# Attention and squared-ReLU layer on one core: the second layer's quarters as a chain in one PSUM region, batch 1's first layer by seven products, and a new order

## The chip, the cores and the metric

The kernel runs on one core of one Trainium2 chip. The metric is the device time of one execution in microseconds; of several runs the median is taken. A profile comes from one execution of its own, and its span goes from the first to the last instruction of the core.

## The reference

Four batches of 768 tokens, eight heads of 64. Each token attends to the last 128 tokens and to the first four ("sinks"); the 512 numbers that come out go through two layers with a squared ReLU between.

```
scores = scale * q @ k.T                       # scale = 1/sqrt(64)
keep   = (pos_k < 4) | (0 <= pos_q - pos_k < 128)
a      = softmax(where(keep, scores, -1e9))
x      = concat_heads(a @ v)                   # [3072, 512]
h      = x @ w_in                              # [512, 2048]
g      = max(h, 0) ** 2
out    = g @ w_out                             # [2048, 512], float32
```

## The kernel before

The work is cut by batch (0 to 3), and each batch of 768 tokens into three slices (or pairs) of 256 tokens. For each batch the kernel loads q, k and v (`qn`, `qr`, `v`), transposes q and k into `qkT` (on TensorE as `pt` for batches 0 and 1; for batches 2 and 3, named `NATURAL`, by DMA "turns" that SP issues), computes scores `ps` (L600, L607), exponentials `expm` on ScalarE (L628), triangle masks on POOL (`domask`, L215), values `po` (L676), normalises them into `xn_sb` (L693), and transposes them into `xT` (L725). Then follow two layers.

**First layer** in its plain form (`layer1`, L757): each block of 128 of the 2048 hidden columns is four matmuls over the depth of 512, `pm`; a relu (L768 on ScalarE, L770 on VectorE) and a square into `gT_sb`. Batches 0 and 1 are done so.

**First layer by seven products** (`layer1_fast` and `quad`, L887), for batches 2 and 3: the depth, the hidden columns and the tokens are each halved, and the eight half-products are replaced by seven of sums and differences (Strassen's scheme). Tokens' sums are `xs` (L845), weights' sums `wi` (L803; two of them are written into `w_in_sb` itself, L811, after the plain layers are through). A quad takes its seven products in one two-bank `pm`, with a copy `t`, two subtractions (L928), a relu (L943), a saturated sum with a floor at zero (L955) and two squares (L909, L911). `FAST = (2, 3)` names the batches.

**Second layer** in its plain form (`layer2`, L976) for pairs (0,0) and (0,1), given as (batch, pair); and by seven products (`layer2_fast`, L1086) for the ten other pairs. Here the two tiles of 128 tokens, the two halves of the 2048 and the two halves of the 512 output columns are the halves. Four sums of `gT_sb` blocks are made on VectorE (`total`, L1044: s1 to s4), four of `w_out_sb` once (`wt`). The seven products p1 to p7 (eight matmuls of 256 columns each) go into four half banks a, b, c, d of two PSUM banks; five additions behind them give the four quarters of `osb`:

- p5 goes to c, is copied into `osb` (x), and p7 in d is added to that (`pair_sum`, L1111)
- p1 goes to a and is copied into `u`; p6 goes to b, and is added to u (L1111)
- x + u is one quarter (L1127); p3 is added in c and p4 in d on the PE, and u is added to both (`middle`, L1134)
- p2 is added to a, which is copied out.

The last pair, (3,2), has a tail form of it with halved copies and stores.

**The order.** Every operation is entered in a plan with the operations it must follow and the buffers ("rooms", `Slot`) it takes. `ORDER` then lists all by number, in the order in which they are issued; a letter names the engine where there is a choice (d VectorE, a ScalarE, g POOL), and `+0`, `+1` the kind of room. Each engine takes its instructions in that order. `DUMMIES` adds matmuls without use ahead of a few operations near the start. PSUM has two rooms of two banks named `att` and two named `den`; the SBUF rooms of the pools `qr`, `qs`, `expm`, `r`, `osb`, `sg`, `u` are few: five `qr`, three `r`, two `osb`, four `sg`, two `u`. `touch` declares which PE and non-PE accesses to one two-bank tile lie in other banks, so that they don't wait for each other.

`load_natural` loads batches 2 and 3 into `qr` rooms and turns them by DMA. `weight_sums_in` makes the `wi`, which live in two of the `qr` rooms for good.

Of the kernel before, what the change touches and what calls it, by code (L numbers as in the profile page):

```python
# [21 lines left out]
0 7 8 9 1 5 10 11 2 12 13 3 14 15 55d 57+0 16 19 59a 20 17 56d 21 18 61d 63+0 22 58 62d 65a 60d 64 6 67a 83+1 79 66a  # L22
68d 69+1 85 70 71d 103+0 84+0 105 73g 74d 72d 23 75+1 86 76 77d 91+0 78a 24 87+1 93 25 89 88 92+0 80 26 114+1 90 94
95+0 4 96 117 97 106g 99+1 98 104+0 107 100d 101 118g 81+1 102d 113+0 108d 156 115 127 27 28 29 30 31 32 33 34 35 36
37 38 116d 82 109+0 111 39 40 41 119+1 121 157a 158a 110 112 120 122 162 123+1 125 163d 168 169d 126a 124a 171 172a
170a 159 160d 177 128 131 165 173d 161d 132d 178d 166d 164a 130a 129a 133a 144 146 136 138 174 145 137 289 290 148
134 175a 140 135 176a 147d 167d 139d 291 179d 292 293 141d 142 143 149g 42 43 44 45 46 150 151 47 48 49 50 51 52 53
54 365 366 367 368 208g 369 370 371 372 373 294 295 152 154 296 153d 155d 297d 298d 186 187d 180 181a 200+0 204+1
192+0 201 193 205 194a 206d 195a 189 207d 182d 203a 196+0 197 183 198a 190a 191a 188d 199d 202d 274 212+0+0 184d 209
278 279 215 213 237+0+0 210+1 211 238 240 185d 300 301 275 214 302 241d 276 277 303 280 281 282 304 219+0+0 283 222  # L30
220 306a 305 307 230+0+0 309a 233 231 308 311 223 216 221 310 239d 224+0 312 234g 232g 299 385 386 384 383 313 225
314 242+0 217+0 243 218 284 315 316 235+0 236 285 251+0 286a 287a 317d 252d 253d 244+0 246 226+1 228 247d 227d 245a
248+1 229a 399 322 249d 250d 402 400 323d 355 401 256+0+0 259 257 340 254+0 255 341a 258d 358 356 342a 396 260d 334
335a 374 375 376 377 378 379 380 381 395g 388 390 387 288 392 391 318 389 393 394 331 263+0+0 332a 261+1 264 266 319
262 267d 324d 406 333a 407 320a 337 409 265g 382 597 268+0 598 599 600 601 602 603 604 605 606 607 608 609 610 338a
321d 403 269 328 627d 410 270+0 272 404 408 329a 271a 273d 359 325 405 339a 336a 326a 346 347d 357 327a 415 418 419d
330d 352 411 353a 416 412 354d 447 448 343 344a 345a 349 422 423 425 417g 426g 611 451 452 397 363 449 453d 350d 398
450 351a 348a 454 455 457 466 456a 438 458 459 441 439 467 485 486 489 490 487 460 488 461 361 492 431 491a 432 434
615 413 616 622 620 619 493 462 494d 468 463 464a 414 465 621 617 618 420 440g 612 424g 427 496 433g 442g 428 498
421 470 471 443 435g 436 472a 504a 495 362 499 497 500 473 444 437 508 505 469 628 501 475d 474 477 647 429 625 445  # L40
430 446 650 502a 648 624 503 623 626 360 476 478 481 507 479 506 480 364 482 483d 523+0 525a 524 631 527 526 528 634
632 509+0 510 529 511d 512 530 531a 654 538 633 539 513 514 515 655 533 534 657 649g 656g 516 517a 638 613 614 535
635 536d 537 641 519 520 532a 636 658g 651g 521 639 569+0 570 637 571a 629 583+0 630 572 573 585a 640 522a 518a 574
584 587 575 576 586 555+1 642 589 577a 588 643 679 557a 540 556 590 559 591a 592a 578a 558 560 579 580 593 594 581
561 562 595 541+0 542 683 563a 564a 543d 545 544 680 546 565 547 566 548 684 686 644 567 685a 596a 549a 582a 681
550d 689 682 645 484 646 670 551 552 687 690 673 671 674g 553 688a 554a 663 691 694 666 664 665g 568d 698 692 693
699 659 652 702 703 705 667g 672g 695 696d 700 653 717 660 718 721 668 697 661 736a 704a 669 737 675 676 701 722 739
740 738 708 677 678 662 755+1 706 709 741+1 742 757a 719 720 756 743a 723a 707d 759 745 724 758 761 725 744 760 762
763a 764a 711 746 727 710 713 726a 765 766 747 712 769 714 771 767 728 730 715d 772 748 749a 729 815+0 816 817a 732
770 731 818 733 819 751 752 787+1 734a 735 716 801+0 802 803a 789a 753 820 804 768d 821 788 822 773+1 805 791 754a  # L50
823a 824a 775a 790 806 750d 792 829 807 774 793 776 825 808 794 826 809a 827 830 831 795a 796a 810a 777 779 811 778
812 797 798 833 780 834 836 813 799 828a 835a 781a 832 838d 839 783 784 782a 800a 814a 837 840 841 844 785 786d 842
848 849 852 853 855 843 845 846d 867 854a 850 851 858 857d 868 871 847 856 859 873a 861 862 860 863 864 869 872 865a
866 870 877 874 876a 875 878 880 881 886 879 882 883 885 884
# [59 lines left out]
def kernel(  # L114
# [81 lines left out]
    def touch(t, e, ins, *banks, alone=False):  # L196

        before = touched.setdefault(t, [])
        for e_, ins_, banks_, alone_ in before:
# [3 lines left out]
        before.append((e, ins, banks, alone))  # L203
# [178 lines left out]

    def load_natural(b, s, older_values):
# [36 lines left out]
    def attention(b, key):  # L420
# [3 lines left out]
        begun = [ops["layer1", b - 1, 0, 0]] if b >= 2 and b not in NATURAL else []  # L424
# [12 lines left out]
        def stage(g, f0, f1, side):  # L437
# [100 lines left out]
            if g == 0:  # L538
                def sink_keys(e):
                    for h2 in range(2):  # L540
                        r = slice(64 * h2, 64 * h2 + 64)
                        nc.vector.tensor_copy(
                            out=kb[r, :].rearrange("p (m c) -> p m c", c=136)[:, :, 4 * h2:4 * h2 + NSINK],
                            in_=qkT_sb[r, :, 1, 0, 0:NSINK])
# [11 lines left out]
                A["sink_keys"] = op(at(0.1), {"dve": 0.34}, sink_keys,  # L556
# [189 lines left out]
    def layer1(b, key, fbs, c0, cw, need):  # L746
# [3 lines left out]
        bs, rs = Slot("den", 1), Slot("r", 1)  # L750
# [10 lines left out]
        ops["layer1", b, fbs[0], c0] = a  # L761

# [51 lines left out]
    def layer1_fast(b, ss, key, step):  # L814
# [15 lines left out]
        if len(ss) == 1:  # L830
            landed = [op(key(0) - 0.012, {"act": 1.06, "dve": 1.2}, spread, after=landed, takes=[whole])]
# [28 lines left out]
    def quad(b, ss, qd, key, xs, sums, slots, part, landed, whole):  # L860
# [15 lines left out]
        def product(name, bk, n, fresh, after):  # L876
# [19 lines left out]
            ops["layer1", b, (f0, name), ss[0]] = o  # L896
            return o
# [19 lines left out]
        m1 = product(1, 0, 0, True, [o for x, o in ops.items() if x[0] == "layer1" and x[1] == b - 1])  # L917
# [43 lines left out]
    def layer2(b, u, keys, by_part=False):  # L961
        P.group = ("l2", b, u)
        bs = Slot("den", 2)
# [57 lines left out]
    def layer2_fast(b, u, key):  # L1021
# [33 lines left out]
        bs, os_, us = Slot("den", 1 if tail else 2), Slot("osb", 1), Slot("u", 1)  # L1055
        ys = Slot("att", 1) if tail else bs
# [84 lines left out]
        pairs = out[128 * g:128 * g + 256, :].rearrange("(i p) m -> p i m" if b in FAST and u else "(p i) m -> p i m", i=2)  # L1141
# [23 lines left out]
        def store_rest(e):  # L1165
            o = bank_t["osb", b, u]
            if b not in FAST or not u:
# [15 lines left out]
    NATURAL, TURNED, BIASED, FAST = (2, 3), (), 1, (2, 3)  # L1183
# [24 lines left out]
    for b in range(B):  # L1208
        if b == 0:
# [3 lines left out]
            at(1, 0.2, 0.725, "att")  # L1213
# [4 lines left out]
        elif b in FAST:  # L1218
            layer1_fast(b, (0,), lambda i, b=b: b + 0.167 * i / 2, 0.01)
            layer1_fast(b, (1, 2), lambda i, b=b: b + 0.167 + 0.34 * i / 4, 0.01)  # L1220
        else:
            for i, fb in enumerate(range(0, NFB, 2)):
                layer1(b, b + 0.34 * i / 8, (fb, fb + 1), 0, 512, (0, 1))
        for i, fb in enumerate(range(0, NFB, 4) if b not in FAST else ()):
            if b == 0:
                layer1(b, 0.2 + 0.226 * i / 4, range(fb, fb + 4), 512, 256, (2,))
            else:
                layer1(b, b + 0.34 + 0.167 * i / 4, range(fb, fb + 4), 512, 256, (2,))
        if b + 1 == FAST[0]:
            weight_sums_in(b + 0.4, [ops[x] for x in ops if x[0] == "layer1" and x[1] == b])  # L1230
        if b + 1 < B:
# [7 lines left out]
            else:  # L1239
                attention(b + 1, lambda f, b=b: b + LO + (HI - LO) * f)(0, 0.0, 1.0, "att")  # L1240
        if b == 0:
            weight_sums(0.6, [w_out_op[i] for i in range(4)])
        for u in range(NS):
            if b == 0 and u < 2:
# [40 lines left out]
```

## Time and profile before

| what | value |
|---|---|
| median of 3 runs | 213.55 us (212.48 to 214.01) |
| profiled execution: span | 210.2 us, 5719 instructions, mean TensorE clock 0.997 |
| TensorE busy | 201.4 us (96%) |
| VectorE, ScalarE, POOL busy | 170.8, 126.6, 101.8 us |
| DMA | 26.09 MB in 93881 packets, mean 124 GB/s |
| first scores of batch 2 | at 72.7 us |
| batch 1's first layer | 73.1 to 99.6 us, between other work |
| pair (0,2)'s second layer begins | at 58.7 us |

The profiled execution has no time beside its span; the span lies 3.35 us under the median of the runs and 2.3 under the fastest. Busy time counts each instruction from its start to its modelled end, so neighbouring matmuls overlap in their records: eight matmuls of 256 columns stand 0.87 us from the next group, though one has a mean of 273 ns. Idle time of an engine other than the bounding one costs nothing by itself.

### The profile page before, as it was taken

Reading aid. Unit: us, or ns where it says so; the run is one execution under the profiler, and the core shown is the slowest. Engines: PE = TensorE matmul, PEld = TensorE weight load, DVE = VectorE, ACT = ScalarE, POOL = GpSimd, SP = SyncE. Lnnn points to the kernel's source line nnn. Section 1 sums busy time; section 2 is a strip of 40 time slices with the busy share of each in tenths; the row PEclk is TensorE's granted clock in tenths of the full one; section 3 lists DMA queues with packets and bytes.
Section 4 is the critical chain, followed back from the end, with each engine's and each line's share of the span. In section 5 each row is a group of like instructions: output and inputs, shape, how many; then the busy total and the mean of one; then the engine's idle time right before and its main releaser. Section 6 shows DMA issues by size and latency. Waiting matters only on the chain.

```text
span 210.2 us, 5719 instructions
## 1 busy us (share of the span) xinstructions
PE 201.4 (96%) x2383; PEld 169.4 (81%) x2383; DVE 170.8 (81%) x317; ACT 126.6 (60%) x162; POOL 101.8 (48%) x143
## 2 busy tenths in 40 slices
PE   3999999999999999999999999799999999999993
PEld 3859996689468845679789988699899999999892
DVE  7487567366999964789997988999989978999863
ACT  2498287407744579898952268889870244896110
POOL 7999774898877941999369023700253000000000
PEclk9999999999999999999999999999999999999998
DMA  5999999999999999999987639700512300400222
GB/s 171 278 188 206 171 201 214 161 155 205 153 112 157 104 150 252 138 124 144 149 102 151 103 77 179 50 3 0 150 62 69 75 5 38 166 0 0 103 100 100
DMA packets 93881, 26.09 MB, mean 124 GB/s; under 512 B 86816, under 2 KB 91552, under 8 KB 93856
## 3 DMA queue, kind: packets, MB, share of 16 engines
q0 software_dynamic: 69248, 12.59, 81.3%
q1 hardware_dynamic: 24424, 13.07, 27.9%
q8 instruction: 18, 0.29, 0.6%
q10 hardware_dynamic: 184, 0.07, 0.1%
q14 instruction: 7, 0.06, 0.1%
HBM read 27.30 MB, written 6.29 MB: 160 GB/s over the span
## 4 chain that ended last, share of the span: by engine, by line
PE 94%; DVE 2%; ACT 1%; POOL 1%; issue 1%; POOLq 0%; DVEq 0%
PE py L1086 29%; PE pm L757 20%; PE pm L887 17%; PE po L676 7%; PE py L976 7%; PE ps L607 6%; PE pt L500 3%; PE pt L182 2%; PE px L725 1%; ACT expm L628 1%; PE ya L1086 1%; PE ps L600 1%; PE pk L566 1%; DVE r L955 1%; DVE gT_sb L911 0%
## 5 line engine op out<-in xcount | busy, mean ns | idle before, releaser
L215 POOL TENSOR_SCALAR_AFFINE_SELECT expm<-expm 128x512 bf16<-128x512 bf16 x42 | 29.2, 724 | 49.5 <-ACT expm L628 24.5
L628 ACT ACTIVATE expm<-ps 128x1024 bf16<-128x1024 f32 (+1 forms) x48 | 43.8, 950 | 12.4 <-PE ps L607 11.3
L757 PE MATMUL pm<-xT,w_in_sb 128*128 128x256 bf16 (+1 forms) x320 | 44.7, 294 | 0.0
L757 PEld LDWEIGHTS <-w_in_sb 128*128 128x128 bf16 x320 | 34.2, 114 | 6.6 <-issue 0.9
L1086 PEld LDWEIGHTS <-gT_sb 128*128 128x128 bf16 x336 | 31.1, 98 | 4.2 <-issue 0.5
L1086 PEld LDWEIGHTS <-sg 128*128 128x128 bf16 x240 | 22.8, 98 | 3.3 <-issue 0.5
L768 ACT ACTIVATE r<-pm 128x1024 bf16<-128x1024 f32 x14 | 14.3, 1022 | 13.5 <-PE pm L757 13.4
L887 PEld LDWEIGHTS <-w_in_sb 128*128 128x128 bf16 x256 | 21.8, 114 | 0.5 <-issue 0.2
L887 PE MATMUL pm<-xs,wi 128*128 128x128 bf16 (+1 forms) x192 | 19.5, 246 | 1.5 <-DVE xs L845 0.9
L1086 PE MATMUL py<-wt,gT_sb 128*128 128x256 bf16 x160 | 20.8, 273 | 0.0
L1086 PE MATMUL py<-wt,sg 128*128 128x256 bf16 x160 | 20.6, 273 | 0.0
L909 ACT ACTIVATE gT_sb<-r 128x1024 bf16<-128x1024 bf16 x18 | 18.4, 1051 | 0.3
L1086 PE MATMUL py<-w_out_sb,gT_sb 128*128 128x256 bf16 x144 | 18.5, 273 | 0.0
L189 ACT ACTIVATE osb<-py 128x256 f32<-128x256 f32 (+1 forms) x15 | 6.2, 410 | 20.3 <-DMA out_dram<-osb 6.0
L770 DVE TENSOR_SCALAR r<-pm 128x1024 bf16<-128x1024 f32 x10 | 12.2, 1222 | 7.5 <-PE pm L757 4.3
L887 PEld LDWEIGHTS <-wi 128*128 128x128 bf16 x192 | 16.4, 113 | 2.2 <-issue 2.1
L693 DVE TENSOR_TENSOR xn_sb<-po,rc 128x512 bf16<-128x512 f32 (+1 forms) x28 | 17.2, 615 | 1.0
L676 PEld LDWEIGHTS <-expm 128*128 128x128 bf16 x352 | 16.3, 97 | 1.4 <-issue 0.5
L676 PE MATMUL po<-v,expm 128*128 128x65 bf16 x352 | 17.3, 193 | 0.1
L943 ACT ACTIVATE r<-pm 128x1024 bf16<-128x1024 f32 x12 | 12.1, 1021 | 8.1 <-PE pm L887 7.9
L928 DVE TENSOR_TENSOR t<-t,pm 128x512 f32<-128x512 f32 x24 | 15.9, 680 | 0.9 <-ACT t L189 0.4
L955 DVE CUSTOM_DVE_ANT_1 r<-pm,t 128x1024 bf16<-128x1024 f32 x12 | 14.5, 1220 | 1.6 <-PE pm L887 1.5
(97 smaller groups left out, 381.9 us busy)
## 6 DMA issues: line engine op xcount, KB each, us to landing
out_dram<-osb SPq DMA_DIRECT2D x11, 512.0 KB, 4.5
v<-in_v_dram POOLq DMA_DIRECT2D x24, 128.0 KB, 7.1
qn<-in_k_dram POOLq DMA_DIRECT2D x20, 128.0 KB, 7.1
qn<-in_q_dram POOLq DMA_DIRECT2D x20, 128.0 KB, 6.9
w_in_sb<-in_moe_w_in_dram POOLq DMA_DIRECT2D x4, 512.0 KB, 10.2
w_out_sb<-in_moe_w_out_dram POOLq DMA_DIRECT2D x4, 512.0 KB, 10.4
qr<-in_k_dram SPq DMA_DIRECT2D x4, 256.0 KB, 5.1
qr<-in_q_dram SPq DMA_DIRECT2D x4, 256.0 KB, 4.8
```

The source lines that it names most:

```text
L215: nc.gpsimd.affine_select(out=e_tile, in_=e_tile, compare_op=ALU.is_ge, fill=fill, base=i - 1, pattern=[[0, n], [1 if i else -1, 128]], ch ...
L628: nc.scalar.activation(out=x[:, :, o:512], in_=bank_t["s", b, s, m][:, :, o:512], func=AF.Exp, scale=scale)
L676: touch(("po", b, s, m0), e, nc.tensor.matmul(pv[:, i, h2, :], lhsT=lhsT, rhs=rhs, start=(n_ == 0), stop=(n_ == len(mms) - 1)), j)
L693: touch(("po", b, s, m0), e, nc.vector.tensor_tensor(out=xn_sb[:, 2 * s:2 * s + 2, 128 * (m0 + j0):128 * (m0 + j0 + nj)].rearrange("p i (j ...
L757: nc.tensor.matmul(pm[:, i, :], lhsT=w_in_sb[:, fb // 4, kb, fb % 4:512:4], rhs=xT[:, c0 // 256:(c0 + cw) // 256, kb, :], start=(kb == 0), ...
L768: nc.scalar.activation(out=o, in_=h, func=AF.Relu)
L887: touch(tag, e, nc.tensor.matmul(y[:, bk, i, :], lhsT=weights(name, f0 + i, a), rhs=rhs[:, a, :], start=fresh and i == 0 and a == 0, stop= ...
L909: nc.scalar.activation(out=d, in_=x, func=AF.Square)
L928: touch(tag, e, nc.vector.tensor_tensor(out=T["t"], in0=T["t"], in1=T["y"][:, bk], op=ALU.subtract), bk)
L955: touch(tag, e, nc.vector._custom_dve(TENSOR_ADD_SAT, out=r.rearrange("p b n c -> p b (n c)"), in0=T["y"].rearrange("p b n c -> p b (n c)" ...
L976: touch((b, u), e, nc.tensor.matmul(pm[:, i, :], lhsT=gT_sb[:, fb, 128 * t:128 * t + 128], rhs=w_out_sb[:, fb, :], start=(fb == 0), stop=( ...
L1086: ins = nc.tensor.matmul(y_, lhsT=x[:, i, :], rhs=r_, start=(first or tail and n == 2) and i == 0, stop=i == HB - 1, skip_group_check=not ...
```

## The change

- Nine of the ten fast pairs get a new form of the second layer, `layer2_chain`; the last pair keeps `layer2_fast`. The same seven products are taken. p1 goes into a half bank r and is copied to the first quarter of `osb`; p6 is accumulated on it and the sum copied to the third; p5 is accumulated and the sum copied to the fourth; p3 is accumulated and the sum copied to the second. p7, then p4, go to half bank d, p2 to half bank a (both in the other bank), and three additions put them onto the quarters. The buffer `u`, L1127 and L1134 are gone for these pairs.
- Batch 1's first layer goes by seven products as well (`FAST` now names, per batch, the slices taken together). Its `wi` are therefore made earlier, after batch 0's first layer, and take their two `qr` rooms from then on.
- All two-bank PSUM users may take either kind of room, `att` or `den`.
- The sink keys are copied by ScalarE where the order says so, before always by VectorE; the spread of a lone slice is on ScalarE only.
- Loads of batches 2 and 3 follow the first operation of the first layer two batches earlier, whichever that is; only those of batch 3 must follow the first `wi`. Attention no longer waits in the plan for the first layer one batch earlier.
- `ORDER` is new: 944 entries for 887. It is left out below.

```diff
-    def touch(t, e, ins, *banks, alone=False):
+    def touch(t, e, ins, *banks, alone=False, part=None):
...
-            apart = (e == "pe") != (e_ == "pe") or e != e_ and alone and alone_
+            apart = (e == "pe") != (e_ == "pe") or e != e_ and alone and alone_ and (part is None or part != part_)
...
-        begun = [ops["layer1", b - 2, 0, 0], w_out_op[3]]
+        begun = [first_layer1[b - 2], w_out_op[3]]
...
-                if b - 1 in FAST:
+                if b == 3:
                     o.after += [ops["wi", 1, 0]]
...
-        begun = [ops["layer1", b - 1, 0, 0]] if b >= 2 and b not in NATURAL else []
+        begun = []
...
-                        nc.vector.tensor_copy(
-                            out=kb[r, :].rearrange("p (m c) -> p m c", c=136)[:, :, 4 * h2:4 * h2 + NSINK],
-                            in_=qkT_sb[r, :, 1, 0, 0:NSINK])
+                        copy(e, kb[r, :].rearrange("p (m c) -> p m c", c=136)[:, :, 4 * h2:4 * h2 + NSINK],
+                             qkT_sb[r, :, 1, 0, 0:NSINK])
...
-                A["sink_keys"] = op(at(0.1), {"dve": 0.34}, sink_keys,
+                A["sink_keys"] = op(at(0.1), {"act": 0.42}, sink_keys,
...
-        bs, rs = Slot("den", 1), Slot("r", 1)
+        bs, rs = Slot(("den", "att"), 1), Slot("r", 1)
...
-        m1 = product(1, 0, 0, True, [o for x, o in ops.items() if x[0] == "layer1" and x[1] == b - 1])
+        m1 = product(1, 0, 0, True, [])
...
+    def layer2_chain(b, u, key):
...
+        o1 = total("s1", a21, a22, ALU.add, s1_, key(0), low + high, [])
+        o3 = total("s3", a11, a21, ALU.subtract, None, key(0), low + [o1], [])
+        o2 = total("s2", "s1", a11, ALU.subtract, s2_, key(0), [o1], [s1_])
+        o4 = total("s4", a12, "s2", ALU.subtract, s4_, key(0), [o2], [s2_])
+
+        bs, os_ = Slot(("den", "att"), 4), Slot("osb", 1)
+        w = lambda half, cols: w_out_sb[:, HB * half:HB * half + HB, 256 * cols:256 * cols + 256]
+        HOME = {"r": (0, 0), "d": (1, 0), "a": (1, 1)}
...
+                for i in range(HB):
+                    touch((b, u), e, nc.tensor.matmul(region(name), lhsT=x[:, i, :], rhs=w_[:, i, :],
+                                                      start=first and i == 0, stop=i == HB - 1,
+                                                      skip_group_check=not first), HOME[name][0])
...
+                d = bank_t["osb", b, u][:, q, :]
+                if add:
+                    ins = nc.vector.tensor_tensor(out=d, in0=region(of), in1=d, op=ALU.add)
+                else:
+                    ins = copy(e, d, region(of))
+                touch((b, u), e, ins, HOME[of][0], alone=True, part=q)
...
+        p1 = product(0, "r", a11, w(0, 0), True, low, takes=[bs])
+        p7 = product(1, "d", "s3", 3, True, [o3, ops["wt", 3]], [p1])
+        c1 = quarter(0, "r", 0, [p1], False, takes=[os_])
+        p6 = product(2, "r", "s2", 2, False, [o2, ops["wt", 2], c1], reads=[s2_])
+        c2 = quarter(2, "r", 2, [p6], False)
+        p5 = product(3, "r", "s1", 1, False, [o1, ops["wt", 1], c2], reads=[s1_])
+        c3 = quarter(3, "r", 3, [p5], False)
+        p2 = product(4, "a", a12, w(1, 0), False, high, [p7])
+        e1 = quarter(0, "a", 4, [p2, c1], True, reads=[bs])
+        e4 = quarter(3, "d", 4, [p7, c3], True)
+        p3 = product(5, "r", "s4", w(1, 1), False, [c3, o4], reads=[s4_])
+        p4 = product(6, "d", a22, 4, False, [e4, ops["wt", 4]] + high)
+        e2 = quarter(1, "r", 5, [p3], False, reads=[bs])
+        e3 = quarter(2, "d", 6, [p4, c2], True, reads=[bs])
...
-    NATURAL, TURNED, BIASED, FAST = (2, 3), (), 1, (2, 3)
+    CHAIN = True
+    NATURAL, TURNED, BIASED = (2, 3), (), 1
+    FAST = {1: ((0, 1), (2,)), 2: ((0,), (1, 2)), 3: ((0,), (1, 2))}
+    CLASSIC2 = ((0, 0), (0, 1))
...
+        if done and 1 not in {x[1] for x in ops if x[0] == "wi"}:
+            weight_sums_in(b + 0.4, [o for x, o in ops.items() if x[0] == "layer1"])
...
-                layer2_fast(b, u, lambda n, u=u, b=b: b + 0.5 + 0.5 * (8 * u + 8 * n / 7.0) / 24)
+                (layer2_chain if CHAIN and (b, u) != (B - 1, NS - 1) else layer2_fast)(
+                    b, u, lambda n, u=u, b=b: b + 0.5 + 0.5 * (8 * u + 8 * n / 7.0) / 24)
```

More of the change, by code (lines that the diff above doesn't have):

```diff
@@ L27 @@
[L27 to L36, printed above, removed]
@@ L830, in layer1_fast @@
         if len(ss) == 1:
-            landed = [op(key(0) - 0.012, {"act": 1.06, "dve": 1.2}, spread, after=landed, takes=[whole])]
+            landed = [op(key(0) - 0.012, {"act": 1.06}, spread, after=landed, takes=[whole])]
         else:
@@ L1053, in layer2_fast @@
         o4 = total("s4", a12, "s2", ALU.subtract, s4_, key(0), [o2], [s2_])
-        bs, os_, us = Slot("den", 1 if tail else 2), Slot("osb", 1), Slot("u", 1)
-        ys = Slot("att", 1) if tail else bs
+        bs, os_, us = Slot(("den", "att"), 1 if tail else 2), Slot("osb", 1), Slot("u", 1)
+        ys = Slot(("att", "den"), 1) if tail else bs
         w = lambda half, cols: w_out_sb[:, HB * half:HB * half + HB, 256 * cols:256 * cols + 256]
@@ L1139, in layer2_fast @@
         g = NT * b + 2 * u
-        pairs = out[128 * g:128 * g + 256, :].rearrange("(i p) m -> p i m" if b in FAST and u else "(p i) m -> p i m", i=2)
+        natural = any(u in ss and len(ss) == 2 for ss in FAST.get(b, ()))
+        pairs = out[128 * g:128 * g + 256, :].rearrange("(i p) m -> p i m" if natural else "(p i) m -> p i m", i=2)
         def rows(i, c0, c1):
```

148 lines of the change are left out of this document (108 added, 40 removed).

## The prediction

> **What bounds the kernel now.** I read the page's busy shares first, then the chain that ended last, then the waits of TensorE, then the stages in windows, and last the groups by line for prices.
>
> ```profile
> PE 201.4 (96%) x2383; PEld 169.4 (81%) x2383; DVE 170.8 (81%) x317; ACT 126.6 (60%) x162; POOL 101.8 (48%) x143
> ...
> PE 94%; DVE 2%; ACT 1%; POOL 1%; issue 1%; POOLq 0%; DVEq 0%
> ```
>
> ```profile
> PE pt L182 <- POOL ident L239: 3.5, 1, 3.5
> PE pm L887 <- DVE xs L845: 0.9, 1, 0.9
> PE pm L887 <- ACT r L943: 0.7, 1, 0.7
> ```
>
> ```profile
> 16.80:72.70 55.90, 55.87 (x652) 44.97 (x654) 42.11 (x73) 29.95 (x41) 44.61 (x58) 1.00 1.84 167
> 72.70:100.10 27.40, 27.40 (x278) 18.49 (x278) 20.56 (x39) 24.39 (x29) 19.44 (x25) 1.00 2.16 161
> 100.10:123.90 23.80, 23.80 (x309) 20.43 (x308) 21.78 (x45) 12.39 (x17) 10.23 (x14) 1.00 1.02 119
> 123.90:166.40 42.50, 40.96 (x562) 37.55 (x561) 40.15 (x70) 30.22 (x38) 12.88 (x18) 1.00 0.38 75
> ```
>
> ```profile
> L757 PE MATMUL pm<-xT,w_in_sb 128*128 128x512 bf16 x64 | 15.1, 381 | 0.0
> ...
> L943 ACT ACTIVATE r<-pm 128x1024 bf16<-128x1024 f32 x12 | 12.1, 1021 | 8.1 <-PE pm L887 7.9
> L928 DVE TENSOR_TENSOR t<-t,pm 128x512 f32<-128x512 f32 x24 | 15.9, 680 | 0.9 <-ACT t L189 0.4
> L955 DVE CUSTOM_DVE_ANT_1 r<-pm,t 128x1024 bf16<-128x1024 f32 x12 | 14.5, 1220 | 1.6 <-PE pm L887 1.5
> L1044 DVE TENSOR_TENSOR sg<-gT_sb 128x1024 bf16<-128x1024 bf16 x10 | 7.5, 748 | 0.6 <-ACT gT_sb L909 0.5
> L1134 DVE TENSOR_TENSOR osb<-py,u 128x512 f32<-128x512 f32 x10 | 6.9, 689 | 3.3 <-PE py L1086 3.2
> L189 ACT ACTIVATE osb<-py 128x256 f32<-128x256 f32 (+1 forms) x15 | 6.2, 410 | 20.3 <-DMA out_dram<-osb 6.0 <-DVE osb L1134 5.3 <-PE py L976 5.0
> L1127 DVE TENSOR_TENSOR osb<-osb,u 128x256 f32<-128x256 f32 x10 | 5.1, 506 | 0.1
> L1111 DVE TENSOR_TENSOR u<-py,u 128x256 f32<-128x256 f32 x10 | 4.2, 419 | 1.9 <-PE py L1086 1.8
> ```
>
> TensorE is 96% busy and is the chain. The waits answer (total, times, longest) leaves 1.6 us inside the body, both in batch 2's first layer: 0.7 at 131.6 and 0.9 at 133.9. Another 3.5 stand ahead of the first matmul and 3.5 behind the last. In the windows (length, then the busy time of PE, PEld, DVE, ACT, POOL) TensorE is unbroken from 16.8 to 123.9. So a microsecond of products taken out is a microsecond of time, unless something else makes TensorE wait. VectorE is next: it has 40.15 of 42.5 in the stage where the two waits stand, and 20.56 of 27.4 in batch 1's first layer (72.7 to 100.1), the stage that the change makes heavier. In the groups the two last numbers before the idle column are busy time and mean ns; records of neighbouring matmuls overlap, so I price matmuls by the time from one group to the next: eight of 256 columns 0.87, sixteen of 256 1.75, eight of 512 1.73, eight of 128 0.44.
>
> The profiled span is 210.2. The median of the runs, 213.55, lies 3.35 over it; I carry that 3.35 unchanged.
>
> **The change, part by part.**
>
> *Batch 1's first layer by seven products.* Before it is 64 matmuls of 512 columns and 64 of 256 (L757): 64 x 0.216 + 64 x 0.109 = 21.0 us. Seven products of half the blocks and half the depth do 7/8 of that: 18.4. **TensorE: -2.6.** Every price is proportional to columns, so nothing is lost to the smaller shapes.
>
> It is paid for behind TensorE. Each of the six quads (four over two slices, two over one) needs one copy of 0.6 (L189, on ScalarE for five of them), two subtractions of 0.68, one saturated sum of 1.22, one relu of 1.02 and two squares of 1.05. VectorE in this layer: 6 x 1.22 + 12 x 0.68 + 3.4 for the input sums + 0.7 + two squares 1.4 = 21.0, against three relus (3.7) and four squares (2.9) before: +14. The weight sums (L803, L811; ten of 0.68 to 0.79) are done anyway; they only move earlier, into a part where VectorE has 42.1 of 55.9.
>
> *Second layer as a chain.* Nine of ten fast pairs keep their seven products of eight matmuls, 56 x 0.109 = 6.1 us each, so TensorE gains nothing. Behind them the old form has three copies (0.41 each), two pair sums (0.42), L1127 (0.51) and L1134 (0.69): 2.0 us that only VectorE can do. The new has four copies, which go to ScalarE in 29 of 36 places by the order, and three adds of 0.42: 1.26. VectorE gets back 9 x 0.74 = 6.7, and with the copies that move about 8. ScalarE pays about +4. All counted, relus and sink copies too, VectorE goes to about 176 and ScalarE to about 137 of 208: VectorE's share from 81% to 84%.
>
> *What the chain makes TensorE wait for.* Product 6 adds on what product 1 left in the half bank, after a copy has taken it; then product 5, then product 3: three links per pair, 27 in all. A copy takes 0.38 (ScalarE) to 0.41 (VectorE). I summed the rows of the TensorE instructions that the new order puts between the links: the least is 0.65 (batch 1's last pair), four have 0.87, the rest 0.95 to 5.97. Each covers its copy if ScalarE or VectorE takes it at once: **0**. If the copy stands behind one relu (1.02) the short links lose up to 0.6: five such links, up to +3.
>
> *New order, five places.* (1) The two waits of before. The relu behind the 0.7 now has four other products between it and its consumer (I summed 2.0 us); the sum xs behind the 0.9 is made for batch 2 with VectorE freer: **-1.6**, bounds 0 and -1.6. (2) The opening of pair (0,2): the last block of batch 0's first layer goes through relu 1.02, square 0.69, sums s1 and s3 (0.75, 0.72) to its second product: 3.3 with the hand-overs. The order has 2.28 of TensorE work between. **+1.0**, bounds 0 and 1.0. (3) Loads of batch 2. The rooms qr now hold two weight sums for good, and the others come free only with batch 1's last transposes, about 58 us against 50.4 before. Thirteen POOL issues at 0.875 (11.4 us) stand ahead of the triangles (L215) for two value products; they end at about 70.6, just when those products are due. The SP turns behind them then run 1.3 each and end at about 85, landing near 90; the scores (2,0) are due at about 89: **+0.5**, bounds 0 and +7 (the first seven turns of the trace took 14.4 us from 59.2, 2.05 each, which would land them near 96). Queued behind a late turn on SP are the other turns and the stores; nothing on TensorE asks for a store before the end. (4) Batch 1's first layer with its neighbours: between the first and the last of its instructions the order puts TensorE 22.6, VectorE 26.4, ScalarE 22.9. VectorE lags by up to 6.2 there. In the same sums the old order has a lag of 9.2 in one place, with no wait in the trace, as VectorE works ahead elsewhere. **+0.5**, bounds 0 and +3. (5) The tail (last pair) keeps its old form: 0.
>
> Sum: -2.6 - 1.6 + 1.0 + 0.5 + 0.5 = -2.2. Span 208.0, time **211.3**. All low bounds together: 213.55 - 2.6 - 1.6 = 209.3. The high ones: -2.6 + 0 + 1.0 + 3 (links) + 7 + 3 = +11.4, not likely all at once.
>
> [...] The longest pause inside the body is 0.9, and in the window 130 to 135 TensorE is busy 3.46 of 5.00 with the granted clock still 1.00. [...]
>
> **Rivals.**
>
> *A. The saving is kept whole.* Waits vanish and nothing comes in their place: 209.3. For it: 55.87 of 55.90, TensorE fed through a crowded stage. Against: places (2) and (3).
>
> *B. VectorE and ScalarE become the bound of batch 1's first layer.* The 2.6 us taken there come back as waits of L887 for t, r or xs, like the two seen at 131 and 134, where VectorE had 40.15 of 42.50. 26.4 against 22.6 gives at most 3.8; the middle, 1.9, with the rest of the sum on it (-2.2 - 0.5 + 1.9 = -0.8): 212.8, and with the waits of batch 2 kept 213.6.
>
> *C. Slower: the turns of batch 2 are late.* One mechanism, at the first scores of batch 2 (L607): rooms free at 58 instead of 50.4, the turns at 2.05 apiece instead of 1.3, ten of them. 7 us late less the 0.5 in the sum: 211.3 + 6.5 = 217.8. It decides above 1.6 us per turn (three tenths more on ten turns take up what the sum still wins). For: the first seven turns did run at 2.05. Against: these ran beside loads on the same DMA share; turns take 1.22 of SP.
>
> *D. Slower: the chain's copies are exposed.* 27 links x 0.4 = 10.8 if nothing covered them; with half exposed +5.4: 216.7. Against: the order's 0.65 and more, and before, products that also waited for copies (L189 osb, u) show no wait on TensorE in 20 such places. [...]
>
> *E. The products taken out were hidden anyway.* If batch 2's start hangs on POOL's masks and SP's turns and not on TensorE, the 2.6 become a wait at the end of that stage: -2.2 + 2.6 = +0.4: 213.9. For: POOL is the most loaded queue up to 72.7 (44.61 of 55.90). Against: TensorE waited for none of it in the trace.
>
> **How the numbers follow.** Forecast 0.45 (own range 210 to 212.6), A 0.14, B 0.20, C 0.08, D 0.09, E 0.04. What a measurement tells from no change is 1%, 2.1 us: faster is under 211.4, slower above 215.7. Faster: A 0.14 and two thirds of the forecast, 0.30: 0.44. Slower: C and D and a little of B, 0.19. Within: 0.37. The range 208.8 to 216.2 leaves out most of C, half of D and a little below A.
>
> **What would show it.** Right: PE busy near 198.8 with 1.5 to 2.5 of waits in the body; no wait for xs L845 or r L943 at batch 2; a wait near 1 us at the opening of pair (0,2), for sg; no wait of L2 products for osb. Wrong: waits of several us at L607 for a turned qkT (C), many waits of 0.1 to 0.5 for osb copies (D), many at L887 for t, r or xs between 73 and 100 (B), one wait of over 2 us at 95 to 105 for expm or qkT (E).

## The result and the profile after

The changed kernel takes 211.03 us (median of 7 runs, 210.54 to 211.91), the kernel before 212.66 us in the seven runs that belong to the comparison (212.29 to 214.01). The ratio is 0.992 with a 95% interval of 0.990 to 0.994: 1.6 us faster, clear of noise, and inside the 1% that the prediction called "within".

The page of the profiled execution, its first lines and the chain by engine:

```profile
span 208.8 us, 5932 instructions
PE 199.5 (96%) x2475; PEld 174.2 (83%) x2479; DVE 172.7 (83%) x317; ACT 134.0 (64%) x188; POOL 96.9 (46%) x141
...
PE 91%; ACT 4%; issue 1%; POOL 1%; DVE 1%; POOLq 0%
```

TensorE's waits (total, times, longest) and the same stages as in the prediction:

```profile
PE pt L185 <- POOL ident L242: 3.5, 1, 3.5
PE py L1235 <- ACT expm L632: 0.6, 1, 0.6
PE ps L611 <- ACT r L773: 0.4, 1, 0.4
PE po L680 <- ACT expm L632: 0.2, 1, 0.2
```

```profile
16.80:72.70 55.90, 54.64 (x641) 44.06 (x642) 42.29 (x74) 33.53 (x48) 42.53 (x58) 1.00 1.87 170
72.70:100.10 27.40, 27.25 (x369) 25.11 (x367) 26.15 (x47) 26.00 (x38) 21.90 (x30) 1.00 1.93 149
100.10:123.90 23.80, 23.80 (x351) 20.40 (x350) 22.33 (x47) 14.35 (x20) 9.60 (x13) 1.00 1.70 146
123.90:166.40 42.50, 42.50 (x554) 38.51 (x553) 37.95 (x67) 32.13 (x44) 8.99 (x14) 1.00 0.27 70
```

The two waits of batch 2's first layer are gone from this trace: 42.50 of 42.50 where it was 40.96. A new 1.0 us stands in the stage 16.8 to 72.7. TensorE's busy time is 1.9 less than before, 199.5. In the stage that holds most of batch 1's first layer VectorE has gone from 20.56 to 26.15 of 27.40 and ScalarE from 24.39 to 26.00, and TensorE waits there only 0.15. All three are full.

The new wait is the opening of pair (0,2). A stretch of the timeline (start, duration, engine):

```profile
61.86 1.02 ACT L773 ACTIVATE r<-pm 128x1024 bf16<-128x1024 f32 x1 [2.63 <-PE pm L761]
62.78 2.64 ACT L632 ACTIVATE expm<-ps 128x1024 bf16<-128x1024 f32 x3
62.92 0.69 DVE L784 TENSOR_TENSOR gT_sb<-r 128x1024 bf16<-128x1024 bf16 x1
62.94 0.34 PE L611 MATMUL ps<-qkT 64*128 64x256 bf16 x4 [0.40 <-ACT r L773]
63.65 0.69 DVE L1209 TENSOR_TENSOR sg<-gT_sb 128x1024 bf16<-128x1024 bf16 x1
63.85 1.03 PE L1235 MATMUL py<-w_out_sb,gT_sb 128*128 128x256 bf16 x8 [0.57 <-ACT expm L632]
64.37 0.69 DVE L1209 TENSOR_TENSOR gT_sb<-gT_sb 128x1024 bf16<-128x1024 bf16 x1
65.12 1.05 PE L1235 MATMUL py<-wt,gT_sb 128*128 128x256 bf16 x8
```

Both waits name ScalarE: the scores wait for the relu that reads `pm`, the first product for the first of the three exponentials that read `ps`, and each of these gives a PSUM room back. It isn't the last square that the first product waits for: its first weights were loaded at 63.21, before that square ended at 63.61. The path of relu, square and two sums ends with `s3` (written into `gT_sb`) at 65.06, and the second product starts at 65.12, just behind it. So both paths cost about the same here, and free rooms alone would have won little.

Groups of the new form: three additions a pair, and copies mostly on ScalarE.

```profile
L192 ACT ACTIVATE osb<-py 128x256 f32<-128x256 f32 (+1 forms) x30 | 11.8, 398 | 24.8 <-PE py L1235 19.8 <-DMA out_dram<-osb 4.2 <-PE py L982 0.7
L1249 DVE TENSOR_TENSOR osb<-py,osb 128x256 f32<-128x256 f32 x27 | 11.0, 418 | 4.2 <-PE py L1235 4.1
L934 DVE TENSOR_TENSOR t<-t,pm 128x512 f32<-128x512 f32 x36 | 23.8, 683 | 3.7 <-PE pm L892 2.9
```

### The profile page after: what moved, and what is told of

Its sections match the earlier page's. It is cut to its first block, busy times and chain, and to the rows that moved or that the text cites. A ratio compares the mean times of both kernels' runs of the same rounds, so it can differ in the third digit from the quotient of the medians.

```text
span 208.8 us, 5932 instructions
## 1 busy us (share of the span) xinstructions
PE 199.5 (96%) x2475; PEld 174.2 (83%) x2479; DVE 172.7 (83%) x317; ACT 134.0 (64%) x188; POOL 96.9 (46%) x141
## 4 chain that ended last, share of the span: by engine, by line
PE 91%; ACT 4%; issue 1%; POOL 1%; DVE 1%; POOLq 0%
PE py L1235 27%; PE pm L892 26%; PE pm L761 10%; PE po L680 7%; PE py L982 7%; PE ps L611 4%; ACT expm L632 3%; PE pt L185 2%; PE py L1092 2%; PE pt L505 2%; PE px L729 1%; PE ya L1092 1%; ACT qkT L192 1%; PE pk L570 1%; DVE r L961 1%
## 5 line engine op out<-in xcount | busy, mean ns | idle before, releaser
L218 POOL TENSOR_SCALAR_AFFINE_SELECT expm<-expm 128x512 bf16<-128x512 bf16 x36 | 23.5, 685 | 43.3 <-ACT expm L632 39.8
L915 ACT ACTIVATE gT_sb<-r 128x1024 bf16<-128x1024 bf16 x28 | 28.8, 1054 | 2.5 <-DVE r L961 2.3
L892 PE MATMUL pm<-xs,wi 128*128 128x256 bf16 (+1 forms) x288 | 29.2, 246 | 0.1
L934 DVE TENSOR_TENSOR t<-t,pm 128x512 f32<-128x512 f32 x36 | 23.8, 683 | 3.7 <-PE pm L892 2.9
L892 PEld LDWEIGHTS <-wi 128*128 128x128 bf16 x288 | 24.6, 114 | 1.0 <-DVE xs L850 0.4
L961 DVE CUSTOM_DVE_ANT_1 r<-pm,t 128x1024 bf16<-128x1024 f32 x18 | 21.8, 1218 | 0.5 <-PE pm L892 0.5
L761 PE MATMUL pm<-xT,w_in_sb 128*128 128x256 bf16 x192 | 22.0, 273 | 0.1
L892 PE MATMUL pm<-xs,w_in_sb 128*128 128x256 bf16 (+1 forms) x192 | 19.7, 246 | 0.0
L949 ACT ACTIVATE r<-pm 128x1024 bf16<-128x1024 f32 x16 | 16.3, 1023 | 4.1 <-DVE osb L194 2.3
L680 PE MATMUL po<-v,expm 128*128 128x65 bf16 x352 | 17.9, 193 | 0.2 <-ACT expm L632 0.2
L611 PE MATMUL ps<-qkT 64*128 64x128 bf16 (+1 forms) x256 | 14.4, 238 | 0.4 <-ACT r L773 0.4
```

Source lines behind the costliest of these rows:

```text
L218: nc.gpsimd.affine_select(out=e_tile, in_=e_tile, compare_op=ALU.is_ge, fill=fill, base=i - 1, pattern=[[0, n], [1 if i else -1, 128]], ch ...
L611: nc.tensor.matmul(ps[:, h2, o:o + w], lhsT=qkT_sb[r, m, 1, c, :], rhs=qkT_sb[r, m, 0, qb:qb + w // 128, :], start=(i == 0 and not biased) ...
L680: touch(("po", b, s, m0), e, nc.tensor.matmul(pv[:, i, h2, :], lhsT=lhsT, rhs=rhs, start=(n_ == 0), stop=(n_ == len(mms) - 1)), j)
L761: nc.tensor.matmul(pm[:, i, :], lhsT=w_in_sb[:, fb // 4, kb, fb % 4:512:4], rhs=xT[:, c0 // 256:(c0 + cw) // 256, kb, :], start=(kb == 0), ...
L892: touch(tag, e, nc.tensor.matmul(y[:, bk, i, :], lhsT=weights(name, f0 + i, a), rhs=rhs[:, a, :], start=fresh and i == 0 and a == 0, stop= ...
L915: nc.scalar.activation(out=d, in_=x, func=AF.Square)
```

## Experiments

Each set is timed together with the kernel before, on one chip; 212.5 to 212.9 us is its median in these sets. The changed kernel wasn't timed again with them, so differences from its 211.03 of a few tenths say nothing.

**The eighth product back.** In `quad`, batch 1 alone:

```diff
-                for i in range(nb):
+                for i in [*range(nb)] * (2 if b == 1 and name == 1 else 1):
```

> The changed kernel with product 1 of each of batch 1's six quads run twice (the second time over the first), so TensorE has eight products' work there and all else stays. Eight more matmuls of 128 columns, or four of 256, per quad: 6 x 0.437 = 2.62 us. Theory (TensorE is the bound in batch 1's first layer, the gain is its work): about 2.6 us more than the changed kernel's 211.0, 213.6, and the span 211.4. Rival (VectorE and ScalarE are the bound there, so TensorE has spare time in that stage): at most 1 us more, below 212.1.

213.17 us (212.58 to 213.63), ratio 1.002 (1.000 to 1.004): 2.1 us more than the changed kernel. From the first product of the first layer to the last product of all, its trace has 189.6 us against 187.1, 2.5 more, and product by product all of it arises between 76 and 92 us, in this layer. So four fifths of the 2.62 come through in the time and nearly all of it in the trace: work that is taken out of TensorE there is gained.

**A further 2.6 us taken out.**

```diff
+                depth = 1 if b == 1 and name in (6, 7) else 2
                 for i in range(nb):
-                    for a in range(2):
+                    for a in range(depth):
...
-                            start=fresh and i == 0 and a == 0, stop=a == 1,
+                            start=fresh and i == 0 and a == 0, stop=a == depth - 1,
```

> The changed kernel with products 6 and 7 of batch 1's six quads over half of their depth: the other half is left out, 2.62 us of TensorE. Theory (TensorE the bound, but VectorE and ScalarE nearly as full: their sums between the order's places are 26 and 23 against 20 that would be left for TensorE): a part of it comes through, 0.8 to 1.8 us, 209.2 to 210.2, with new waits of L892 for t, r or xs. Rival (VectorE and ScalarE have plenty of room): all 2.6, 208.4. Other rival (they are the bound already): nothing, 211.0.

210.48 us (ratio 0.990, 0.986 to 0.993), five of six runs between 210.16 and 210.71: only 0.5 of 2.62, less than I expected and not to be told from nothing. The profile is of the sixth run, 212.25; its waits can't account for the median, but they show where time comes back:

```profile
PE pm L893 <- DVE t L935: 1.0, 1, 1.0
PE py L1236 <- DVE osb L194: 0.6, 2, 0.5
PE pm L893 <- DVE xs L850: 0.6, 1, 0.6
PE pm L893 <- ACT r L950: 0.4, 1, 0.4
```

Those for `r` and `xs` stand in batch 1's first layer, at 82 and 90 us, as expected; those for `osb` at 119 and 122. The largest, at 131 us, is in batch 2's first layer, which this edit doesn't touch (see the two waits, below).

**More of VectorE in the same layer.** The saturated sum of `quad` made twice for batch 1:

```diff
-            touch(tag, e, nc.vector._custom_dve(
+            for _ in range(2 if b == 1 else 1):
+              touch(tag, e, nc.vector._custom_dve(
```

> The changed kernel with the saturated sum of each of batch 1's six quads made twice on VectorE (6 x 1.22 = 7.3 us more of VectorE's time between 76 and 105 us; the second gives the same values). Theory (in this layer VectorE is at the edge: 26.7 busy of 28 us between 72 and 100, and taking 2.6 us from TensorE there gained 0.5 only): 5 to 7.5 us more, 216 to 218.5. Rival (VectorE is 83% busy over the span and works ahead, so that it absorbs most): at most 2.5 more, below 213.5.

217.19 us (ratio 1.021, 1.017 to 1.024): 6.2 of the 7.3 us, as the theory had it. Its largest new wait of TensorE is this, in batch 1's first layer:

```profile
PE pm L892 <- DVE xs L850: 1.3, 1, 1.3
```

Though its share over the span is 83%, an extra microsecond of VectorE in this layer costs 0.85.

**The links of the chain, with the order kept.** In `quarter`, copies c1, c2 and c3 made twice:

```diff
                     ins = copy(e, d, region(of))
+                    if n in (0, 2, 3):
+                        touch((b, u), e, ins, HOME[of][0], alone=True, part=q)
+                        ins = copy(e, d, region(of))
```

> The changed kernel, its order unchanged, with each of the 27 copies that stand between two links of the chain made twice (the second over the first, 0.38 to 0.42 us each, 11 us in all on ScalarE and VectorE). Theory (in this order every link has other TensorE work behind it, 0.65 at the least, 0.87 at four, 0.95 and more at the others; a doubled copy takes 0.8 and a hand-over): the five short links wait 0.1 to 0.4 each, and ScalarE's load costs a little: 211.3 to 212.8. Rival D (the copies are on the path): half of 11 us or more comes through, 216 and above. Other rival (all covered with room): 211.0.

214.31 us (213.86 to 214.57), 3.3 more: 1.5 beyond the theory's range and 1.7 below the rival's. Its waits name

```profile
PE ps L611 <- ACT es L578: 0.9, 1, 0.9
PE py L1235 <- ACT osb L192: 0.3, 1, 0.3
PE py L1235 <- DVE osb L1249: 0.2, 1, 0.2
PE py L1235 <- DVE osb L194: 0.2, 1, 0.2
```

This is 0.7 us for copies and adds. That view leaves out the short waits, and a wait costs more than its idle time, since the records of neighbouring matmuls overlap (in the kernel with memsets, below, one of 0.97 moves all later starts by 1.13). With the starts of the two traces laid side by side, TensorE falls behind by 0.14 to 0.41 at nine products of the chain, 2.3 us together, and by 1.0 at scores that stand behind ScalarE's longer queue (`es`), which I had put at "a little". So the links have less room than I thought: not five of them but nine show when their copies double, and about a third of the 11 us comes through.

**The parts of the change alone, in orders not made for them.** Two kernels exchange the form of nine pairs and keep the places in the order; two more move the sums, products and evacuations of these pairs as well.

```diff
 nochain:    the changed kernel (in ORDER, other numbers in the same places)
-    CHAIN = True
+    CHAIN = False
 chainonly:  the kernel before, with layer2_chain and touch of the changed one (ORDER likewise)
-                layer2_fast(b, u, ...
+                (layer2_chain if (b, u) != (B - 1, NS - 1) else layer2_fast)(b, u, ...
```

> The kernel before, its order and its plain first layer of batch 1 kept, with nine pairs of the second layer as the chain, in the places of the old form. In two pairs (batch 1's first two) the order then has nothing on TensorE between the link's copy and the product behind it, in one 0.65, in seven links 0.87. Theory (a copy is hidden wherever the order has 0.65 or more behind the product before it): the two bare links wait 0.45 to 0.6 each; the waits of before (0.7, 0.9) stay or shrink with VectorE's relief: 212.0 to 213.7, against 212.7 of the kernel before. Rival D (copies are exposed at many links): 3 to 6 us slower than before.

228.4 us (ratio 1.074, 1.070 to 1.078): 15.8 us slower than before, and both theories missed it.

> The changed kernel, order and seven products kept, with the nine chained pairs of the second layer in their old form, put into the same places of the order (the products in the old form's own sequence). VectorE gets about 7 us more work. Theory (the chain only relieves VectorE, which is not the bound): within 0.7 us of the changed kernel's 211.0. Rival (VectorE's relief by the chain is what took away the waits at batch 2's first layer): 1.5 to 3 us slower, 212.5 to 214, with L892 waiting for xs and r near 130.

226.99 us (1.064, 1.060 to 1.068): also far outside both. Their largest TensorE waits in the body, chain alone first, then the changed kernel without it:

```profile
PE py L1228 <- ACT osb L189: 7.0, 4, 2.5
PE py L1228 <- DVE sg L1202: 2.8, 2, 1.7
PE py L1228 <- DVE osb L1242: 1.1, 2, 0.6
```

```profile
PE py L1092 <- DVE sg L1050: 3.1, 4, 1.1
PE ps L611 <- ACT expm L632: 2.8, 3, 2.1
PE py L1092 <- DVE osb L1117: 1.7, 3, 0.9
PE py L1092 <- DVE gT_sb L1050: 1.5, 3, 0.9
```

A bare link doesn't cost its copy of 0.38 but the queue ahead of the copy, up to 2.5 us. The old form opens with a product that needs a sum, and waits for `sg` where the chain opens with one that needs none. From the first product of the first layer to the last of all the chain-alone kernel has 206.4 us, 16.8 more than before; 11.6 of these are idle time. Another 3.4 go to two stretches of 3.4 us each at half clock. The rest isn't traced. In its timeline and windows (the column before the last two is the granted clock):

```profile
103.64 2.00 ACT L777 ACTIVATE gT_sb<-r 128x1024 bf16<-128x1024 bf16 x2
105.55 0.36 ACT L189 ACTIVATE osb<-py 128x256 f32<-128x256 f32 x1
105.97 1.61 PE L1228 MATMUL py<-wt,sg 128*128 128x256 bf16 x8 [1.95 <-ACT osb L189]
```

```profile
104.00:112.00 8.00, 6.05 (x48) 4.44 (x47) 5.21 (x9) 4.36 (x7) 2.21 (x3) 0.79 0.85 71
128.00:136.00 8.00, 5.93 (x60) 4.74 (x60) 2.54 (x5) 3.99 (x7) 1.76 (x2) 0.79 0.63 144
```

The copy stands behind two squares; TensorE pauses 1.95 us; its next eight matmuls take 1.54 us to the next group in place of 0.87.

The fitted versions change the list of the order alone, for these pairs; in the chain's, for instance:

```diff
-... 144 146 136 138 174 145 137 289 290 148 134
+... 144 146 136 138 174 145 289 290 137 148 134
```

> As the kernel before with the chain alone, but with the sums, products and evacuations of the nine pairs moved in the order, so that each link has at least 0.87 us of other TensorE work behind it (before: two links with nothing). Batch 1's first layer stays plain. Theory (the chain costs nothing where its copies have cover and the engine is free, and is worth nothing on TensorE): the waits of the unfitted order (12.0 us) go to about 1.6, as in the kernel before, and the clock stays up: 211.5 to 213.2, against 212.7 of before. Rival (27 dependent links cost time in themselves): 215 or more.

> As the changed kernel with the old form of the second layer in nine pairs, but with the sums, products and evacuations of these pairs moved in the order until each opening product has its sum in time as far as that goes. Theory (the old form asks for its first sum ahead of its first product and takes 0.7 us more of VectorE per pair, but neither bounds when the order allows for it): 211.0 to 213.0. Rival (with batch 1 by seven products VectorE is so full that without the chain's relief the saving is gone): 213.5 to 216, with waits of L892 and L1092 for VectorE's t, xs, sg.

221.03 us (1.038, 1.034 to 1.043) and 222.37 us (1.046, 1.042 to 1.049). About half of the loss went with the chain and a third without it, but neither theory held. The largest wait of the fitted chain is this:

```profile
110.73 5.33 DVE L1202 TENSOR_TENSOR sg<-sg,gT_sb 128x1024 bf16<-128x1024 bf16 x1
110.78 4.73 POOL L215 TENSOR_SCALAR_AFFINE_SELECT expm<-expm 128x512 bf16<-128x512 bf16 x8
116.31 0.68 DVE L1202 TENSOR_TENSOR gT_sb<-gT_sb 128x1024 bf16<-128x1024 bf16 x1
117.96 0.42 DVE L1242 TENSOR_TENSOR osb<-py,osb 128x256 f32<-128x256 f32 x1
118.44 1.03 PE L1228 MATMUL py<-wt,gT_sb 128*128 128x256 bf16 x8 [2.67 <-DVE osb L1242]
```

A sum that takes 0.69 elsewhere took 5.33, about as long as eight of POOL's masks and itself, and the addition that the product needs came 2 us behind it in VectorE's queue. A stretch at half clock follows here too (0.64 granted between 120 and 124). What the chain is worth by itself, with an order planned for it, stays open: these runs show only that each form needs its own.

**Does POOL's work off the path cost time?** 28 masks, or 34 memsets, on a spare tile behind POOL's last mask:

```diff
+                                pool_masks.append(1)
+                                if len(pool_masks) == 18:
+                                    nc.gpsimd.memset(spare, 1.0)
+                                    for _ in range(28):
+                                        triangles(spare, 0, 4)
```

> The changed kernel with POOL, idle after 160 us, given 28 more masks of 0.63 to 0.69 us on a spare tile that nothing else reads (18 to 19 us, 160 to 178). No engine waits for them. Some 13 of VectorE's instructions with two SBUF inputs (sums L1209, xs L850, squares L917) stand in that stretch. Theory (such an instruction and a POOL instruction that reads SBUF exclude each other, as in the order-fitted kernel where a sum of 0.69 took 5.33 beside eight masks of 4.73): each is lengthened by 0.3 to 0.7 us, one or more by a whole train; the time grows by 2 to 12 us. Rival (POOL's work off the path is free): 211.0, within 0.5.

213.77 us (212.43 to 214.42, 12 runs; ratio 1.004, 1.002 to 1.006): 2.7 us more, though nothing waits for POOL. Beside the changed kernel's trace, product by product, TensorE falls behind by 2.1 us between 176 and 184, beside the masks and just behind them, at products that wait for VectorE; another 1.1 arises at 130, before the first of them (see the two waits, below). The same group between 160 and 181 us, in the changed kernel and in this one:

```profile
L850 DVE TENSOR_TENSOR xs<-xT 128x512 bf16<-128x512 bf16 (+1 forms) x4 | 1.7, 484 | 0.0
```

```profile
L857 DVE TENSOR_TENSOR xs<-xT 128x512 bf16<-128x512 bf16 (+1 forms) x4 | 3.2, 870 | 0.0
```

```diff
-                                    nc.gpsimd.memset(spare, 1.0)
-                                    for _ in range(28):
-                                        triangles(spare, 0, 4)
+                                    for _ in range(34):
+                                        nc.gpsimd.memset(spare, 1.0)
```

> As the kernel with more POOL masks, but with 34 instructions that only write the spare tile (memset) in place of masks. [...] Theory by this: the time stays at 211.0, within 0.5, and the sums keep 0.68 to 0.70. Rival (any busy POOL holds VectorE up): 2 us or more, as with the masks.

No run before this one had shown what memsets do to these sums. 211.28 us (ratio 0.993, 0.991 to 0.995): no difference from the changed kernel's 0.992, and this group has 485 ns, not 870. POOL is as long busy with the memsets (17.9 us) as 28 masks of 0.64 would be. So here the masks, which read their tile, hold these sums up (870 ns for 484), and the memsets, which only write it, don't (485).

**The tail.** The last entries of the order as before:

```diff
-... 939 937 938 940 941 943 942
+... 939 937 938 943 940 942 941
```

> The changed kernel with the last four entries of the order as in the kernel before: the stores of the last quarter and the middle are issued ahead of the copies and stores of the first quarter, not behind them. Between the last product and the end of the span lie 4.2 us in the changed kernel's trace, 3.5 in that of before. Theory (the two stores of SP at the very end are issued one behind the other, the last 1.4 us after the last product): 0.5 to 0.7 us less than 211.0, that is 210.4. Rival (the landing of stores varies by itself): no difference beyond 0.2.

210.72 us (ratio 0.991, 0.988 to 0.994). From the last product to the end its trace has 3.6 us instead of 4.2, as before the change, so the last entries of the order set that stretch; in the same trace 0.5 was lost at batch 2's first layer. The 0.3 in time can't be told from none.

**A better order?** The operations of the changed kernel, moved for the short openings; the first lines of the list:

```diff
-... 156+0 127 115 82 116d 109+1 111 112 157a 27
-28 29 30 31 32 33 110 119+0 121 158a 34 35 36 37 38 120 39
+... 156+0 82 127 27 28 109+1 29 111 30 115 116d
+119+1 110 31 121 162+0 32 112 33 34 120 123+1 35 36 37 38
```

> The changed kernel with the order alone changed: the tail as in the kernel before, and entries moved so that the opening of pair (0,2) has its square and sums earlier (the two waits of 0.4 and 0.6 there), and the short openings in batches 1 to 3 get more cover. All operations are the same, the TensorE work too. Theory (after the change only 1.2 us of waits in the body and 0.7 of tail are left to win): 0.8 to 1.9 us less than 211.0: 209.1 to 210.2. Rival (VectorE and ScalarE are so full around batch 1's first layer that waits only move): 210.5 to 212.

220.5 us (1.036, 1.032 to 1.040), 9.5 more than the changed kernel, though all the work is the same. It begins here:

```profile
46.00:56.00 10.00, 7.13 (x86) 4.35 (x84) 5.24 (x9) 1.21 (x3) 8.83 (x15) 0.98 2.27 121
```

TensorE is idle for 2.9 of these 10 us: some 0.9 at transposes that now stand ahead of the landing of their loads, 1.9 at two value products that wait for POOL's masks. A stretch at half clock follows at 55.6 (0.6 granted in the page's slice from 54.9 to 60.4). Both theories missed it. None of these versions beats the changed kernel by more than noise.

## Why the prediction was right, step by step

- **TensorE, -2.6.** Confirmed by the eighth product (+2.1 in time, +2.5 in the trace). From the first product of the first layer to the last of all, with every term in it, the trace has 189.6 before and 187.1 after, -2.5 where the sum had -2.2. The terms as they are measured here add up to some -3.0, so half a microsecond is in none of them: busy time fell by 1.9, to 199.5, not to the 198.8 that the prediction named. Counted from start to start, the products of the first layers do take 2.6 less, and TensorE's other work takes about 0.6 more, a part of which is what waits cost beyond their idle time; the rest stays open.
- **The two waits, -1.6.** Gone from the changed kernel's trace, but not for good. In five of the seven other traces with this order up to there, TensorE waits 0.4 to 1.0 us at the same layer, for a subtraction `t`. In these five one turn of `qkT` on SP's queue took 1.8 to 2.1 us (1.2 in the three others), the turn of `xT` behind it landed late, and `xs` waited for it in VectorE's queue ahead of `t`. So the term lies between -0.6 and -1.6 by the execution. The chain alone doesn't bring it: both kernels with the chain in the old order still have the two waits of 0.9 and 0.7. That the new order does, and not the products of batch 1, isn't shown.
- **Opening of pair (0,2), +1.0.** The size and the place are right, the step isn't quite. The sum had the second product wait for `s3`, through relu, square and sums; that path is as long as forecast (3.2 us), but TensorE lost its 0.4 and 0.6 ahead of it, at the scores and the first product, for PSUM rooms that ScalarE gives back. The sign that the prediction named, a wait for `sg`, isn't there.
- **The chain's links, 0.** No wait for `osb` in the changed kernel. Doubling the copies opened 2.3 us at nine links, so they have cover, but little to spare. Rival D's price is refuted for this order, but its mechanism is real: 7.0 us at four places in the order before.
- **Loads of batch 2, +0.5.** The step was too cautious. First load at 58.5 as predicted; the turns went at 1.31 apiece but for two, 1.49 on average, under the 1.6 from which rival C would decide. The tenth was issued at 82.9 and landed at 86.2, 3.0 us ahead of the scores at 89.2. Rival C is out.
- **VectorE and ScalarE in batch 1's layer, +0.5.** 0.15 in that stage. Rival B's mechanism lies right behind the result: 2.6 us less for TensorE gains 0.5 at most, 7.3 us more for VectorE costs 6.2.
- **The tail, 0.** It took 4.2 us instead of 3.5: +0.7. The form is the old one, but the last entries of the order aren't.
- **The base.** Here the prediction erred: it carried 3.35 us from span to median. In the runs listed the time is 1.7 to 2.0 over the span of the same execution, mostly 1.7, so the span of 210.2 belongs to a time of about 211.9, and the three runs gave a median that the later sets put at 212.5 to 212.9. From there -2.2 would have been 210.5. The forecast's 211.3 came nearer because two errors met: a base 0.9 too high, and 1.2 us that the sum didn't have, 0.7 in the tail and 0.5 at the start (which varies by more than that between executions). That it hit to 0.3 is luck; that TensorE's products are the gain is not. The bound of 211.4 for "faster" hung on the same base.

## What to carry to other kernels

Where TensorE bounds the whole, price a change by its columns first, then look in its own stage for what is second: here VectorE's share of 83% over the span said little, and 26.15 of 27.40 in one stage said it. A link through a copy costs the queue ahead of that copy (up to 2.5 us in the chain-alone kernel), not the copy (0.38), so a dependent chain and its issue order are one design. One trace in which a wait is gone doesn't show that it stays away: look for it in every kernel that shares the order. Hold an execution's time against its own span before adding a difference to a median.

## What was not expected of the hardware

- **VectorE and POOL.** Sums with two SBUF inputs and POOL's masks delayed each other here: 0.69 became 5.33 beside eight masks that began 0.05 us after it, in the same kernel as above, and the mask's 0.64 became 1.08 in several places. In the kernel with 28 more masks the group of `xs` sums above took 870 ns for 484, while additions and subtractions with one input in PSUM kept their time (415 for 419 into `osb`, 682 for 683 into `t`), and beside the memsets the same sums took 485. In the case of 5.33 the sum ended 0.55 us behind the whole train of eight (4.73 us). The 28 masks behind POOL's last one didn't repeat that: no sum beside them took more than 1.12. What makes the difference stays open.
- **The clock.** In the chain-alone kernel a pause of 1.95 us was followed by half pace (1.54 us for eight matmuls in place of 0.87), yet one of 2.47 at 180 to 182 in the same run wasn't. The changes of the granted clock in its trace lie on a grid of 3.41 us: down at 106.27, up at 109.68, down at 130.16, up at 133.57. In the kernel before, full clock was granted from 7.60 to 208.99 us, 59 times 3.41. TensorE's busy time in four cells of that grid and in the one behind the first:

```profile
102.85:106.27 3.42, 1.47 (x15) 1.07 (x12) 3.39 (x5) 2.83 (x4) 1.96 (x3) 1.00 1.50 150
106.27:109.68 3.41, 3.41 (x25) 2.11 (x24) 1.55 (x3) 1.48 (x3) 0.00 (x0) 0.50 0.95 99
126.75:130.16 3.41, 1.10 (x18) 0.73 (x16) 0.73 (x3) 2.21 (x3) 0.35 (x1) 1.00 0.44 77
177.95:181.36 3.41, 1.97 (x28) 1.77 (x26) 3.23 (x8) 1.37 (x2) 0.00 (x0) 1.00 0.12 25
181.36:184.77 3.41, 2.38 (x28) 2.21 (x28) 0.00 (x0) 1.75 (x4) 0.00 (x0) 1.00 0.02 5
```

  The pause at 182 is cut by an edge of the grid into 1.44 and 1.03. In all 14 traces, up to the last product, the seven cells with 1.89 us or more of idle time are each followed by one at half clock, where half of 3.41 us, 1.7, is lost, and the others, with at most 1.54, by none. So in these traces half clock followed the idle time of a whole cell, and not the length of one pause. The kernel before has that cell of 1.54: its two waits stand in it together.
- **The start.** In nine kernels with the same opening order the first product of the first layer came between 16.7 and 18.0 us, though their first matmul came at 3.5 in all. The full clock was granted between 6.3 and 8.6; the three with an early clock and a late first product wait 0.7 to 1.0 us for a cast, `qs`. The spread of the first product, 1.3 us, is as large as most effects here, and one reason why one trace can't settle them.
